# Sixteen kept score units instead of twelve, and q and k loaded as a pair, in a fused top-k attention and MLP kernel

## The chip, the cores and the metric

The kernel runs on one core of one Trainium2 chip. The metric is device time in microseconds for one launch; a time is the median of several runs, and one further execution was taken by the hardware profiler. The engines are named as in the profile: PE is TensorE (matmul), PEld its weight load, DVE is VectorE, ACT is ScalarE, POOL is GpSimd, SP is the engine whose queue issues all DMAs here.

## The reference, cut to what matters

```python
batch, n_heads, seq, head_dim = (8, 8, 576, 64)
scores = scale * np.matmul(q, k.transpose(0, 1, 3, 2))
kth = np.partition(scores, -32, axis=-1)[..., -32:-31]
scores = np.where(scores >= kth, scores, -1000000000.0)
scores = scores - np.max(scores, axis=-1, keepdims=True)
attn = np.exp(scores)
attn = attn / (np.sum(attn, axis=-1, keepdims=True) + 1e-09)
x = (attn @ v)            # (B,H,S,D) -> (B*S, H*D) = (4608, 512)
h = x @ w_in              # 512 -> 2048
return np.maximum(0.01 * h, h) @ w_out   # 2048 -> 512
```

The inputs q, k and v are float32, the weights are float64; the result is (4608, 512) float32.

## The kernel before, in words

**Units.** Two heads of a batch form a pair; there are 32 pairs. A unit is 128 rows of queries of both heads of a pair (or 64 rows of two pairs), with all 576 keys: a score tile `s_sb` of 128 x 2 x 576. There are 144 units, 18 for each of the 8 batches. Whole units run over the pairs of a batch within one block of rows, so units n and n + 8 of a batch lie two blocks apart.

**Steps.** The order of work is written out by hand: `for s in range(len(steps) + LAG + 1)`. Step s runs `top_k` of unit s on DVE, `mask` of unit s - 1 on POOL, `exponents` and `sums` of unit s - 1 on ACT (`ze` at L323), and for unit s - 2 the `reciprocals` on DVE (`rz`, L327), `normalize` on ACT (L330) and `transpose`. `transpose` splits the tile into high and low halves on ACT (`split`, L339), stores each to DRAM (`apart`, L340) and reads it back through a transposing DMA (`wT`, L344). For four units near the start (`HASTY`) the transposition is made by PE instead. Two units' value matmuls (`weigh_values`, L381) come some three to five steps after their top-k; `keep_values` (L395) puts the result into `x`.

**Scores.** At the end of each even step, `scores` makes the scores of units s + 2 and s + 3 on PE (L225) and ACT copies them out (L232). Its PSUM buffers are two called `wide` and one called `narrow`, shared with the early scores below and, the wide ones, with the values.

**MLP.** A chunk of 256 tokens (128 for the first two) becomes ready when all its values are there. Its matmuls (`ph`, L437, and `pz`, L449) are handed out in small portions between the attention parts, by a budget worked out from what is still to be done (`slot_budget`, `mlp_steps`). Before the loop the weights are loaded as words of 16 bits and put together (`round_weights`).

**Kept units.** Some units' scores are made in the first steps and stored to DRAM. `KEPT` lists first unit numbers: for each entry a, the units a, a + 1, a + 8 and a + 9 are kept. `load_early` loads what they need into one `raw` buffer (two k tiles of 288 KB, four q slices of 64 KB); `score_early`, at the end of a step, calls `keep_scores` as often as `EARLY_SCORES` says for that step. `keep_scores` makes one unit's scores on PE (L276) in two score buffers, copies them on ACT (L280) into one of three areas of the MLP's tile `gT`, not yet in use, and stores them (`kept`, L282):

```python
        ps = [ps_sc.tile([P, 2, 512], F32, name="wide", bufs=2) if (2 * k + i) % 3 else
              ps_sc.tile([P, 2, 512], F32, name="narrow") for i in range(2)]
...
        both = gT.rearrange("p f n -> p (f n)")[:, k % 3 * 2 * S:(k % 3 + 1) * 2 * S]
```

Three steps ahead of its top-k, `fetch_scores` (L287) loads a kept unit back, and the even step that would have made its scores skips them.

**q and k loads.** At the end of a step `load_more` decides whether a further pair's q and k may be loaded, and puts both into the list `waiting`, if that list is empty. A later step takes from the list, just after it has issued the transposing transfer, but only where it has no kept unit to fetch (L651).

**DMA.** All DMAs are issued from SP's queue in program order, so an issue that waits holds back those behind it.

Of the kernel before, what the change touches and what calls it, by code (L numbers as in the profile page):

```python
# [20 lines left out]
def kernel(  # L21
# [13 lines left out]
    nc = tc.nc  # L35
# [65 lines left out]
    def load_weights(n):  # L101
        if n >= NPIECE:
            return
        if not AS_WORDS:
            nc.sync.dma_start(piece(n), weights[n])
            return
        raw_of[n] = raws.tile([P, WCH, 4], U16, name="raw")
        flat = raw_of[n].rearrange("p n w -> p (n w)")
        for m, c0, c1 in ROUNDED:
            if m == n:  # L110
                nc.sync.dma_start(flat[:, 4 * c0:4 * c1], weights[n][:, 4 * c0:4 * c1])
# [63 lines left out]
    waiting = []  # L175
# [75 lines left out]
    def load_early(us):  # L251

        raw = raws.tile([P, WCH, 4], U16, name="raw").rearrange("p n w -> p (n w)").bitcast(F32)
        at = 0
        for pi in sorted({u.pairs[0] for u in us}):
            kt = raw[:, at:at + S]
            nc.sync.dma_start(kt, kT[pi])
            at += S
            for u in us:
                if u.pairs[0] == pi:  # L260
                    early_of[u] = raw[:, at:at + P], kt
                    nc.sync.dma_start(early_of[u][0], qT[pi][:, u.q0:u.q0 + P])
                    at += P
# [3 lines left out]
    def keep_scores(u):  # L267

        k = len(kept_of)
        qt, kt = early_of.pop(u)  # L270
        ps = [ps_sc.tile([P, 2, 512], F32, name="wide", bufs=2) if (2 * k + i) % 3 else
              ps_sc.tile([P, 2, 512], F32, name="narrow") for i in range(2)]
        for half in range(2):
            for i, _, side, _ in u.parts:
                d = slice(side * D, (side + 1) * D)
                nc.tensor.matmul(ps[i][:, half, 0:HS], qt[d, :], kt[d, half * HS:(half + 1) * HS],  # L276
                                 start=True, stop=True)
        both = gT.rearrange("p f n -> p (f n)")[:, k % 3 * 2 * S:(k % 3 + 1) * 2 * S]
        for i in range(2):
            nc.scalar.copy(both[:, i * S:(i + 1) * S].rearrange("p (h n) -> p h n", h=2), ps[i][:, :, 0:HS])  # L280
        kept_of[u] = kept.tile([P, 2 * S], F32, name=f"kept{k}")
        nc.sync.dma_start(kept_of[u], both)  # L282
# [217 lines left out]

    steps = units

    KEPT = (24, 40, 56)
    EARLY_SCORES = {0: 4, 1: 2, 2: 1, 3: 2, 4: 1, 5: 2}

    def unit(n):
        return steps[n] if 0 <= n < len(steps) else None
# [26 lines left out]
    with tc.manual_schedule():  # L534
        last = {p: n for n, u in enumerate(steps) for p in u.pairs}

        to_keep = [[steps[n] for n in (a, a + 1, a + 8, a + 9)] for a in KEPT]
        early_units = {u for us in to_keep for u in us}
        to_load, to_keep = list(to_keep), [u for us in to_keep for u in us]
        assert all(len(u.pairs) == 1 for u in to_keep)  # L540

        def score_early(count):

            for _ in range(min(count, len(to_keep))):
                keep_scores(to_keep.pop(0))
                if len(to_keep) % 4 == 0 and to_load:
                    load_early(to_load.pop(0))

        def load_more(s):

            for of, load, n, lag in ((v_of, load_v, LOADED_V, LAG + 1), (qk_of, load_qk, LOADED + 3, 8)):
                if of is qk_of and to_keep:
                    while len(of) < LOADED:
                        load(len(of))
                    continue
                while len(of) < NPAIR and (len(of) < n or last[len(of) - n] + lag <= s):
                    if of is v_of or len(of) < n:
                        load(len(of))
                    else:
                        if not waiting:  # L560
                            load(len(of), at_once=False)
                        break


        for n in range(3):
            load_weights(n)
        jobs = [round_weights(*job) for job in ROUNDED] if AS_WORDS else [iter(())] * len(ROUNDED)
        for n in range(len(jobs) + 1):
            if n == len(jobs) - 1:
                first = first_scores(steps[0])  # L570
                next(first, None)
            for job in jobs[max(n - 1, 0):n + 1][::-1]:
                next(job, None)
            if n == len(jobs) - 1:
                next(first, None)
                load_v(0)
                load_v(1)
            elif n == len(jobs):
                for _ in first_scores(steps[1]):
                    pass  # L580
            if n:
                load_weights(n + 2)
            if n >= len(jobs) - 2:
                load_early(to_load.pop(0))
            if 0 <= n - len(jobs) + HP + 1 < HP:
                load_qk(n - len(jobs) + HP + 1)

        def weights_of(u):
            reciprocals(u)
            normalize(u, 0)  # L590
            normalize(u, 1)

        def values(*place):
            due = [u for n, u in enumerate(steps) if values_at(n) == place]
            if due:
                po = ps_sc.tile([P, 2, 512], F32, name="wide", bufs=2)[:, 0, 0:2 * P]
                po = po.rearrange("p (u n) -> p u n", u=2)
            else:
                return ()
            for n, u in enumerate(due):  # L600
                weigh_values(u, po[:, n, :])
            return [(u, po[:, n, :]) for n, u in enumerate(due)]

        def keep(weighed, *place):
            for u, po in weighed:
                keep_values(u, po)
            attended(*place)

        for s in range(len(steps) + LAG + 1):
            assert s < 7 or not to_keep  # L610
            cur, old, older, new = unit(s), unit(s - 1), unit(s - 2), ()
            if s % 2 == 0:
                new = [u for u in steps[s + 2:s + 4] if u]
            picks = top_k(cur) if cur else iter(())
            budget = slot_budget(s)

            def slot():
                next(picks, None)

            at_first = s < HURRY and s - 2 in HURRIED  # L620
            if at_first:
                weights_of(older)
            slot()
            if old:
                mask(old, 0)
                mask(old, 1)
            late = s < HURRY and not {s - 1, s - 2} & set(HURRIED)
            if older and not late and not at_first:
                weights_of(older)
            mlp_steps(budget)  # L630
            weighed = values(s, MIDDLE)
            at_once = s - 2 in HASTY or any(at == (s, MIDDLE) for at, _ in ready_at)
            if at_once:
                keep(weighed, s, MIDDLE)
            slot()
            if older and late:
                weights_of(older)
            if s - 2 in HASTY:
                transpose_in_haste(older)
            mlp_steps(budget)  # L640
            if old:
                exponents(old, 0)
            mlp_steps(budget)
            if older:
                keep_transposed(older) if s - 2 in HASTY else transpose(older, lambda: mlp_steps(budget))
            if not older or s - 2 in HASTY:
                mlp_steps(budget)
            if unit(s + 3) in early_units:
                fetch_scores(unit(s + 3))
            elif waiting:  # L650
                nc.sync.dma_start(*waiting.pop(0))  # L651
            slot()
            slot()
            mlp_steps(budget)
            if old:
                exponents(old, 1)
                sums(old)
            mlp_steps(budget)
            if not at_once:
                keep(weighed, s, MIDDLE)  # L660
            if new and new[0] in early_units:
                new = ()
            if new and s < HURRY:
                scores(new)
            keep(values(s, END), s, END)
            if new and s >= HURRY:
                scores(new)
            score_early(EARLY_SCORES.get(s, 0))
            budget = slot_budget(s + 1)
            mlp_steps(budget)  # L670
            load_more(s)
        mlp_steps(1e9)
# [58 lines left out]
```

## Time and profile before

| What | Value |
|---|---|
| Time before, median of 3 runs | 1464.72 us (1464.65 to 1465.21) |
| Profiled execution, its own time | 1463.63 us |
| Its span in the profile | 1461.7 us |
| PE busy | 1405.5 us (96%) |
| DVE busy | 1320.3 us (90%) |
| ACT busy | 1100.9 us (75%) |
| POOL busy | 1097.8 us (75%) |
| DMA queue of SP, share of 16 engines | 58.5% |
| kept stores and fetches | 12 and 12, 576 KB each |

The span is the time from the first to the last instruction that was profiled; the execution's own time has 1.9 us around it. Busy shares are averages over stages that differ: the first 61 us are weights, from 61 us on the steps run, and after about 1370 us only MLP work is left. PE's matmuls are pipelined and their ends are modelled, so a busy PE is not PE at its peak; its waits say more than its busy time.

### The profile page before, as it was taken

How to read it: one execution, taken by the hardware profiler on the slowest of the kernel's cores; microseconds unless marked ns; L12 is line 12 of the kernel's file. 1: busy time of each engine (PE TensorE's matmuls, PEld its weight loads, DVE VectorE, ACT ScalarE, POOL GpSimd, SP SyncE). 2: the span in 40 equal slices, each digit the busy share in tenths (PEclk: the TensorE clock that was granted, in tenths of full speed). 3: DMA queues.
4: the chain of work that ended last, by engine and by line, in shares of the span. 5: the costliest groups of instructions: out<-in, count | busy, mean ns of one | idle time of the engine just before them, and what ended most of it. 6: DMA issues, size and time to landing. Idle time of an engine off the chain costs nothing.

```text
span 1461.7 us, 24213 instructions
## 1 busy us (share of the span) xinstructions
PE 1405.5 (96%) x8066; PEld 932.9 (64%) x8068; DVE 1320.3 (90%) x3401; ACT 1100.9 (75%) x1984; POOL 1097.8 (75%) x744
## 2 busy tenths in 40 slices
PE   7848999999989999999999999999999999999998
PEld 2425548576757676767676767676766666666674
DVE  7999999999999999999999999999999999999600
ACT  8878878677868777777778787777777777777710
POOL 3288888878888888888888787888887878787700
PEclk9968999999999999999999999999999999999999
DMA  8967543646576666676656655666566665554510
GB/s 320 344 219 225 140 119 101 194 128 181 151 192 179 172 167 188 156 194 169 157 163 170 169 138 141 171 164 166 149 156 171 164 151 143 153 141 130 150 43 14
DMA packets 394989, 239.03 MB, mean 164 GB/s; under 512 B 334576, under 2 KB 336112, under 8 KB 392944
## 3 DMA queue, kind: packets, MB, share of 16 engines
q1 hardware_dynamic: 394864, 237.48, 58.5%
q8 instruction: 63, 1.03, 0.3%
q14 instruction: 62, 0.51, 0.1%
HBM read 55.77 MB, written 99.09 MB: 106 GB/s over the span
## 4 chain that ended last, share of the span: by engine, by line
PE 77%; DVE 13%; ACT 4%; DMA 4%; issue 1%; SPq 0%; POOL 0%; DVEq 0%; ACTq 0%; POOLq 0%
PE pz L449 30%; PE ph L437 29%; PE wide L381 10%; DVE tops L301 5%; PE wide L225 5%; DVE pairs L304 4%; PE narrow L225 3%; DMA apart<-split 2%; ACT split L339 1%; DVE pairs L296 1%; DMA raw<-in_weights_dram 1%; ACT s_sb L318 1%; ACT s_sb L330 1%; DVE w_out L156 1%; DMA wT<-apart 1%
## 5 line engine op out<-in xcount | busy, mean ns | idle before, releaser
L314 POOL TENSOR_SCALAR pen<-s_sb,tops 128x576 f32<-128x576 f32 x288 | 638.3, 2216 | 203.8 <-DVE tops L301 135.6
L301 DVE MAX8 tops<-pairs 128x8 f32<-128x288 f32 (+1 forms) x1152 | 635.9, 591 | 0.0
L449 PE MATMUL pz<-w_out,gT 128*128 128x512 f32 x1152 | 505.1, 595 | 2.4 <-ACT scale L410 2.4
L437 PE MATMUL ph<-x,w_in 128*128 128x256 f32 x2176 | 482.6, 381 | 0.0
L304 DVE MATCH_REPLACE8 pairs<-tops,pairs 128x288 f32<-128x288 f32 (+1 forms) x864 | 460.1, 538 | 0.0
L437 PEld LDWEIGHTS ph<-x,w_in 128*128 128x128 f32 x2176 | 409.5, 190 | 75.5 <-issue 21.3
L315 POOL TENSOR_TENSOR s_sb<-s_sb,pen 128x576 f32<-128x576 f32 x288 | 406.9, 1413 | 24.0
L449 PEld LDWEIGHTS pz<-w_out,gT 128*128 128x128 f32 x1152 | 216.4, 190 | 266.2 <-issue 261.2
L339 ACT COPY split<-s_sb 128x1152 uint16<-128x1152 uint16 x280 | 309.5, 1146 | 1.7 <-DMA apart<-split 1.7
L330 ACT ACTIVATE s_sb<-s_sb,rz 128x576 f32<-128x576 f32 x288 | 207.7, 773 | 33.4 <-DVE rz L327 33.4
L318 ACT ACTIVATE s_sb<-s_sb,nbias 128x576 f32<-128x576 f32 x288 | 222.4, 772 | 6.4 <-POOL s_sb L315 6.4
L296 DVE TENSOR_TENSOR pairs<-s_sb 128x576 f32<-128x576 f32 x288 | 213.6, 780 | 9.5
L381 PEld LDWEIGHTS wide<-wT,vt 128*64 128x64 f32 x3200 | 161.2, 139 | 53.0 <-issue 36.2
L381 PE MATMUL wide<-wT,vt 128*64 128x128 f32 (+1 forms) x3200 | 179.0, 268 | 10.3 <-DMA wT<-apart 4.7
L443 ACT ACTIVATE gT<-ph 128x512 f32<-128x512 f32 x136 | 80.7, 593 | 58.6 <-PE ph L437 57.7
L395 ACT COPY x<-wide 128x128 f32<-128x128 f32 (+1 forms) x160 | 32.2, 260 | 120.2 <-PE wide L381 120.2
L232 ACT COPY s_sb<-wide 128x704 f32<-128x704 f32 x130 | 98.0, 754 | 20.1 <-PE wide L225 20.1
L458 ACT COPY o_sb<-pz 128x512 f32<-128x512 f32 x36 | 21.1, 585 | 92.3 <-PE pz L449 92.2
L225 PE MATMUL wide<-kt,qt 64*128 64x352 f32 (+1 forms) x360 | 70.4, 507 | 1.0 <-ACT s_sb L247 0.7
L232 ACT COPY s_sb<-narrow 128x448 f32<-128x448 f32 x130 | 62.9, 536 | 1.2 <-PE narrow L225 0.6
L304 DVE MATCH_VALUE_LOAD pairs<-tops,pairs 128x8 f32 x864 | 62.6, 72 | 0.0
L327 DVE RECIPROCAL rz<-ze 128x2 f32<-128x2 f32 x144 | 22.3, 155 | 42.3 <-ACT ze L323 42.1
(67 smaller groups left out, 678.0 us busy)
## 6 DMA issues: line engine op xcount, KB each, us to landing
apart<-split SPq DMA_DIRECT2D x280, 288.0 KB, 2.1
raw<-in_weights_dram SPq DMA_DIRECT2D x15, 1024.0 KB, 6.9
vt<-in_vk_dram SPq DMA_DIRECT2D x32, 320.0 KB, 3.7
out_dram<-o_sb SPq DMA_DIRECT2D x36, 256.0 KB, 2.8
kept<-gT SPq DMA_DIRECT2D x12, 576.0 KB, 3.2
s_sb<-kept SPq DMA_DIRECT2D x12, 576.0 KB, 4.8
qt<-in_qT_dram SPq DMA_DIRECT2D x20, 288.0 KB, 3.5
kt<-in_kT_dram SPq DMA_DIRECT2D x20, 288.0 KB, 3.4
```

Source lines behind the costliest of these rows:

```text
L225: nc.tensor.matmul(to[r0:r0 + u.rows, i, :], qt[d, u.q0:u.q0 + u.rows], kt[d, k0:k1], start=True, stop=True)
L296: nc.vector.tensor_tensor(pairs[:, :, n, :], u.both[:, :, 0:HS], u.both[:, :, HS:S], op)
L301: nc.vector.max(out=u.tops[:, i, r, :], in_=rest[i])
L304: nc.vector.match_replace(out=rest[i], in_to_replace=u.tops[:, i, r, :], in_values=rest[i], imm_value=LOWEST)
L314: nc.gpsimd.tensor_scalar(pen, u.s[i], u.tops[:, i, ROUNDS - 1, 7:8], MASKED, ALU.is_lt, ALU.mult)
L315: nc.gpsimd.tensor_tensor(u.s[i], u.s[i], pen, ALU.add)
L318: nc.scalar.activation(u.s[i], u.s[i], AF.Exp, bias=u.nbias[:, i:i + 1], scale=SCALE, accum_out=u.z[:, i:i + 1])
L330: nc.scalar.activation(u.s[i], u.s[i], AF.Copy, bias=0.0, scale=u.rz[:, i:i + 1])
L339: nc.scalar.copy(split, pairs[:, :, h])
L381: nc.tensor.matmul(po[side * D:(side + 1) * D, o, :], vt[:, c, side, :], u.wT[:, c + side * NKC if c + 1 < NKC else c, r:r + n], start=(c ...
L437: nc.tensor.matmul(ph[:, i, 0:n], w_in[c][:, f * P:(f + 1) * P], x[c][:, 0:n], start=(c == 0), stop=(c == HP - 1),)
L449: nc.tensor.matmul(pz[0:m, 0:DMODEL], gT[:, f, r0:r0 + m], w_out[f // 4][:, f % 4, :], start=(f == 0), stop=(f == NFC - 1),)
```

## The change

The diff adds a fourth entry to `KEPT`, so that the units 72, 73, 80 and 81 are kept too. `EARLY_SCORES` makes sixteen units in steps 0 to 5 in place of twelve: five, four, one, three, one and two, where there were four, two, one, two, one and two. A fourth `load_early` follows in step 0, after the first four units, since `score_early` loads another group whenever the number still to make is a multiple of four. Where a step has no unit to fetch, it now issues all that `waiting` holds, which is the q and the k of one pair, and not one of them.

```diff
-    KEPT = (24, 40, 56)
-    EARLY_SCORES = {0: 4, 1: 2, 2: 1, 3: 2, 4: 1, 5: 2}
+    KEPT = (24, 40, 56, 72)
+    EARLY_SCORES = {0: 5, 1: 4, 2: 1, 3: 3, 4: 1, 5: 2}
...
             if unit(s + 3) in early_units:
                 fetch_scores(unit(s + 3))
-            elif waiting:
-                nc.sync.dma_start(*waiting.pop(0))
+            else:
+                while waiting:
+                    nc.sync.dma_start(*waiting.pop(0))
```

## The prediction

> **What bounds the kernel now.** I read the page first, then the chain of waits, then windows, then single engines. The page's chain by engine says that TensorE (PE) carries the end, with VectorE (DVE) second:
>
> ```profile
> PE 77%; DVE 13%; ACT 4%; DMA 4%; issue 1%; SPq 0%; POOL 0%; DVEq 0%; ACTq 0%; POOLq 0%
> ```
>
> 77% of a span of 1461.7 us is not one stretch. In time order the chain runs through DVE and ACT until about 260 us, alternates until 431, and is nearly pure PE from there. The waits of PE from 432 us to the end (the window cuts the first one, which ends at 431.6) say the same:
>
> ```profile
> PE wide L381 <- DMA wT<-apart: 4.2, 1, 4.2
> PE wide L381 <- DMA vt<-in_vk_dram: 0.3, 1, 0.3
> ```
>
> So after 431.6 us PE work taken away is time taken away, and in the first 140 us PE work is nearly free. What is not free there is ScalarE (ACT). In the chain of the first 140 us, the stretch from 83.5 to 138.3 is ACT, with PE and DMA between its pieces; it ends when ACT's sum (ze) lets DVE's reciprocal go on:
>
> ```profile
> 83.52 0.08 DVE rz L327
> 83.63 1.44 ACT s_sb L330 x2
> ...
> 127.67 6.86 DMA apart<-split
> 134.57 0.04 issue
> ...
> 138.34 0.17 DVE rz L327
> ```
>
> DVE's timeline shows 1.62 us idle before that last reciprocal. The steps before it had 0.7 to 5.3 us between ze and rz, so this is the first time that ACT's lateness stops DVE. From 138 to 206 us DVE runs 8.87 us a step without a gap, so a later start there is a later everything.
>
> **What the skill says.** "DMA: Bandwidth & Descriptors", Queues, rings and completion order: an SDMA engine consumes a ring's descriptors in order. The trace agrees: the last load issued at 74.8 us, behind three v loads and a q, took 5.1 us to land, while a kept store took 2.8 at its shortest. The same page, Specifications, gives about 358 GB/s to HBM per core; the window 61.4 to 74 us shows 325 at a DMA share of 0.91, so that queue is already close to full. "TensorE: Matmul & The Clock Gate", What's actually happening: an idle PE drops to half clock after about 3.4 us. The window 74 to 110 us shows a granted clock of 0.63, so early scores run slower than the same matmuls late.
>
> **Gain.** Units 72, 73, 80, 81 no longer have their scores made at the ends of steps 70 and 78. One pair of units there costs, in the chain:
>
> ```profile
> 308.07 0.79 PE wide L225 x4
> 308.87 0.76 PE narrow L225 x8
> 309.62 0.59 PE wide L225 x4
> ```
>
> That is 2.14 us a pair, 4.28 for two. A check by windows cut at the value matmuls of units 40, 72 and 104, 32 units each; the first has three pairs of kept units (steps 46, 54, 62), the second none:
>
> ```profile
> 467.18:757.07 289.89, 289.89 (x1734) 198.59 (x1733) 283.36 (x738) 226.47 (x419) 240.42 (x161) 1.00 0.65 173
> 757.07:1052.96 295.89, 295.56 (x1777) 202.26 (x1776) 282.08 (x736) 232.79 (x427) 239.10 (x161) 1.00 0.58 157
> ```
>
> 6.00 us over three pairs is 2.00 a pair, with four fetches' traffic and more in it. I take **4.2 us** for two, with 3.2 to 4.6 as bounds. It can be kept only if DVE follows: DVE needs 16 x 8.87 = 141.9 us for steps 72 to 87, and those steps take 148.5 now, so there are 6.6 us of room. The four new fetches (s_sb<-kept, 576 KB, 4.8 us to land) come in steps 69, 70, 77, 78, behind the transposing transfer, and delay the next split store. Units 69 and 77 now have their transposed weights 3.3 us before PE wants them; the units at the same place behind the older fetches (45, 53, 61) have 0.04, 2.4 and 1.4, and PE waited at none of them. That is in the lower bound.
>
> **Early cost.** Step by step, on ACT. An early unit is two copies of 0.64 us; they are 1.18 together, plus PE's turn-round in the three score buffers.
>
> Step 0 gets a fifth unit. Its copies end near 74 us; ACT then idles until 77.1 for GpSimd's mask, which hides it. The fourth early load also comes here: six SP issues of 0.3 to 0.45 us, 832 KB, ahead of three v loads and a q and k which nobody needs before about 111 us. Cost on the path nothing, but these bytes stand in the ring.
>
> Step 1 has four units for two. ACT's timeline now, with the idle at the end:
>
> ```profile
> 78.09 0.62 ACT L280 COPY gT<-wide 128x576 f32<-128x576 f32 x1
> 78.61 0.64 ACT L280 COPY gT<-narrow 128x576 f32<-128x576 f32 x1
> 80.14 0.64 ACT L280 COPY gT<-wide 128x576 f32<-128x576 f32 x1 [0.89 <-PE wide L276]
> 81.08 0.64 ACT L280 COPY gT<-wide 128x576 f32<-128x576 f32 x1 [0.30 <-PE wide L276]
> 83.63 1.44 ACT L330 ACTIVATE s_sb<-s_sb,rz 128x576 f32<-128x576 f32 x2 [1.91 <-DVE rz L327]
> ```
>
> Two units took 3.6 us. The first of the four has its matmuls done early; three more at 1.7 to 1.9 each end near 84.7, so L330 starts 1.1 us late. There is also a wait that is not there now: the stores leave from three buffers in gT, and the fourth unit of step 1 must wait for the landing of the first one's store, issued near 79.4 behind the fifth store, the early load and the v, q, k loads. From 72 us that is 3.6 MB; at 325 GB/s the ring is clear of loads near 83.5, and the store lands near 85. L330 then starts at 86.3, 2.7 late. I take **2.5**; bounds 1.0 and 4.0. Queued behind the waiting copy on ACT are the normalisation, exponents and splits of unit 0, hence SP's stores and DVE's reciprocals of later units.
>
> Step 3 has three units for two: 1.18 of copies and 0.3 of turn-round, **1.5**, bounds 1.2 and 2.0. Step 4 keeps its one unit, but the rotation of score buffers now gives it wide first, narrow second. Today PE begins it only when ACT has freed the narrow buffer (4.5 us idle at 109.47); the wide half can go ahead, one matmul of 0.5 to 0.9 us sooner: **-0.7**, bounds -1.0 and 0. Steps 2 and 5 keep counts; step 5's own copies lie beside SP, which is what ends it.
>
> Sum 2.5 + 1.5 - 0.7 = **3.3 us** of lateness at unit 3's split stores in step 5. SP then issues the transposing transfer, two stores, six q/k loads and the next split store (the 6.86 us landing), all in the same order as now, and rz of unit 6 comes 3.3 later. Earlier reciprocals stop DVE first (slack 2.0 and 0.7 us in steps 4 and 6), which is the same delay, not a second one. Nothing later gives it back: DVE has no idle to use up, and PE waits for these units. Bounds of the sum 1.2 to 6.
>
> **Pairs of q and k.** No bytes are added; the k load moves one step forward, and later pairs up to six steps. Each adds one SP issue of 0.43 us and 288 KB, about 0.8 us of ring, ahead of the next split store. SP's gaps there (it waits 392 us in all for ACT's splits) hide the issue. The tightest units after such a load, 41 and 43, have 1.2 and 1.5 us of slack, so I take **0**; if that cover were gone, up to 0.8 once or twice. A gain from earlier q and k is 0, since L225 never waits for a load. The while loop adds no wait, and GpSimd's queue is untouched.
>
> **Sum.** -4.2 + 3.3 = **-0.9 us**. The profiled execution took 1463.63 (span 1461.7 and 1.9 around it), 1.1 below the median of 1464.72; from it 1462.7, from the median **1463.8**. About 0.2%, 2.9 us, is what a measurement of this kernel can tell from no change.
>
> **Rivals.**
> A. *Tie*, as summed: 1463.8, own range 1461.8 to 1465.6. Chance 0.47.
> B. *The early work is hidden.* The fifth store lands in time and step 3 meets PE turn-round that was idle anyway: lateness 1.2, 1461.7, or 1461.1 with the gain's upper bound. For it: 7.4 us of ACT idle in steps 1 and 2, and a store of 2.8 us if the ring is not full. Against it: most of that idle is PE's turn-round on ACT's own copies and moves with them. Chance 0.35.
> C. *The store buffer becomes the bound*, slower. If the ring in step 1 runs at 200 GB/s, as the 36 us from 74 run on average (212), 3.6 MB last until 90, the store lands at 91.5, L330 starts 9 us late, and the sum is about 9.8 - 4.2: 1470. It decides when that landing is later than 88.8 us, 9.4 after issue; the longest of the twelve stores now took 5.6. Chance 0.11.
> D. *New fetches starve PE* as at 431.6 us, where a fetch and a v load came together: 4.2 us for one of the two pairs, 1468. The v loads lie in steps 72 to 75, not beside them. Chance 0.07.
> That the change does not do what it says is excluded by its order of instructions: sixteen kept stores, four more fetches, pairs of loads.
>
> Range 1460.6 to 1467.0. A falls wholly within 0.2%, apart from its ends; faster 0.36, same 0.45, slower 0.19.
>
> **What would show it.** Right: 16 instructions each in L282 and L287; the last copy of step 1 waiting for a DMA or PE, and L330 of unit 0 starting between 84.5 and 88; rz of unit 6 near 141.6; PE's first unbroken stretch starting near 435; 32 units from the values of unit 72 near 291.8 us. Wrong: rz of unit 6 still at 138 to 139 (B), a copy in step 1 idle for 5 us or more (C), a new PE wait for wT near units 69 to 81 (D).

## The result: slower by 0.4%, and the profile after

| | median | range | runs |
|---|---|---|---|
| before | 1464.68 us | 1461.89 to 1465.85 | 6 |
| after | 1469.73 us | 1467.18 to 1473.69 | 6 |

The ratio is 1.0037, with a 95% interval of 1.0022 to 1.0053: the kernel became 5 us slower where a gain of 0.9 us was forecast, with 1467.0 us as the upper end of the range. A second measurement of the same kernel, among the experiments (e9), gave 1.0027 (1.0016 to 1.0038).

The first profile of after was taken of its slowest execution (1473.69 us, span 1471.9), the second (e9) of one of 1468.34 (span 1466.5). Both are used below.

The page's chain by engine, after, against the first fence of the prediction:

```profile
PE 77%; DVE 11%; DMA 5%; ACT 4%; issue 1%; POOL 1%; SPq 0%; DVEq 0%; POOLq 0%; ACTq 0%
```

PE has the same share; DMA takes a point and DVE gives two. Where the DMA part lies is told by the chain of waits of after, from 79 to 93 us (start, length, what):

```profile
81.63 0.46 ACT gT L280
82.09 7.96 DMA kept<-gT
90.05 0.02 issue
...
90.68 0.65 ACT gT L280
91.32 1.34 ACT s_sb L330 x2
```

A kept store is on the path that sets the end: issued at 82.09, landed at 90.05. ACT's timeline in step 1 shows who stood behind it; the brackets give the idle time before the row and what ended it:

```profile
84.64 0.64 ACT L280 COPY gT<-narrow 128x576 f32<-128x576 f32 x1 [0.30 <-PE narrow L276]
90.14 1.18 ACT L280 COPY gT<-wide 128x576 f32<-128x576 f32 x2 [4.86 <-DMA kept<-gT]
91.21 1.45 ACT L330 ACTIVATE s_sb<-s_sb,rz 128x576 f32<-128x576 f32 x2
```

The fourth early unit of step 1 waited 4.86 us for a free area. Before, L330 started at 83.63 and had waited for DVE; now DVE waits for ACT. DVE's waits from 60 to 160 us, before and then after (second trace), as total, times and longest:

```profile
DVE rz L327 <- ACT ze L323: 1.6, 1, 1.6
```

```profile
DVE rz L327 <- ACT ze L323: 9.5, 6, 2.8
```

The late gain is there. Windows between the value matmuls of units 56, 72 and 88, before and then after (length, then the busy time of PE and the other engines; the last three figures are PE's granted clock, the DMA share and GB/s):

```profile
611.64:757.07 145.43, 145.43 (x818) 99.72 (x817) 141.61 (x369) 113.90 (x209) 119.90 (x81) 1.00 0.63 168
757.07:904.55 147.48, 147.48 (x865) 100.52 (x864) 140.69 (x368) 115.82 (x211) 119.23 (x81) 1.00 0.57 153
```

```profile
624.69:767.98 143.29, 143.29 (x802) 98.28 (x801) 141.29 (x369) 111.52 (x205) 119.72 (x81) 1.00 0.67 178
767.98:914.13 146.15, 145.56 (x850) 99.05 (x849) 140.55 (x368) 113.32 (x207) 119.08 (x81) 1.00 0.60 163
```

2.14 us less in the first and 1.33 in the second, where PE waited 0.59 for the transposed weights of unit 81.

**Where the time went, stretch by stretch.** Each row is the length in one trace less the length in the trace of before, in us. Steps are cut at the first MAX8 of their unit on DVE, values at their first matmul on PE.

| Stretch | after | after, 2nd | pairs alone (e1) | four areas (e3) | fourteen (e11) |
|---|---|---|---|---|---|
| start to step 0 (weights) | +1.5 | +0.3 | +0.7 | -0.4 | +0.6 |
| step 0 to step 9 | **+8.3** | **+8.3** | -1.0 | +4.0 | -1.7 |
| step 9 to step 40 | +0.7 | -1.1 | -1.0 | -0.7 | -1.8 |
| step 40 to values of unit 40 | +1.9 | +1.5 | +0.9 | +1.2 | +1.4 |
| values of units 40 to 56 | +0.6 | -0.1 | +0.1 | -0.1 | -0.1 |
| 56 to 72 | -2.1 | -2.1 | 0.0 | -2.1 | -2.1 |
| 72 to 88 | -1.3 | -1.9 | 0.0 | -1.3 | 0.0 |
| 88 to the end | +0.7 | 0.0 | -0.5 | +0.2 | +0.4 |
| span | +10.2 | +4.9 | -0.9 | +0.7 | -3.3 |

The pairs-alone kernel takes the same time as before, so its column shows what single traces differ by: about 1 us a row. Rows of that size are not explained. The row from step 40 to the values of unit 40 is longer than before in every other trace (0.5 to 1.9 us), also in e12 (+1.6), which has neither more kept units nor pairs of loads: there the one trace of before is short. What stands out is the stretch from step 0 to step 9 and the two kept windows.

**ACT's lateness.** The start of `normalize` (L330) of units 0 to 6 after the first MAX8, less the same before. A normalisation of unit n lies in step n + 2, so column 0 holds what step 1 added, column 2 less column 1 what step 3 added, and so on. Step 1 is the same code in after and e5, and in e3 and e6; their 6.1 and 5.0, 1.8 and 1.2 show how far single traces differ.

| Kernel | 0 | 1 | 2 | 3 | 4 | 5 | 6 |
|---|---|---|---|---|---|---|---|
| after | 6.1 | 6.1 | 8.2 | 7.6 | 9.6 | 9.5 | 9.3 |
| after, 2nd (e9) | 6.2 | 6.2 | 7.7 | 7.2 | 9.3 | 9.5 | 9.2 |
| four areas (e3) | 1.8 | 1.8 | 3.4 | 2.9 | 5.0 | 5.1 | 4.9 |
| loads later (e4) | 2.0 | 2.0 | 3.6 | 3.1 | 5.1 | 5.2 | 5.5 |
| rotation (e5) | 5.0 | 5.0 | 6.8 | 6.2 | 6.2 | 6.8 | 7.3 |
| both (e6) | 1.2 | 1.1 | 3.2 | 2.7 | 2.7 | 2.7 | 2.6 |
| six, three (e7) | 0.0 | 0.0 | 2.1 | 1.5 | 1.5 | 1.4 | 1.2 |
| six, four (e10) | 0.9 | 0.3 | 0.3 | -0.2 | -0.2 | -0.2 | -0.1 |
| fourteen (e11) | 0.0 | 0.0 | 0.0 | 0.0 | -1.5 | -1.9 | -1.6 |

### The profile page after: what moved, and what is told of

It reads as the page before. It is cut to its first block, busy times and chain, and to the rows that moved or that the text cites. A ratio compares the mean times of both kernels' runs of the same rounds, so it can differ in the third digit from the quotient of the medians.

```text
span 1471.9 us, 24274 instructions
## 1 busy us (share of the span) xinstructions
PE 1411.2 (96%) x8066; PEld 936.7 (64%) x8068; DVE 1320.4 (90%) x3401; ACT 1100.6 (75%) x1984; POOL 1096.3 (74%) x744
## 4 chain that ended last, share of the span: by engine, by line
PE 77%; DVE 11%; DMA 5%; ACT 4%; issue 1%; POOL 1%; SPq 0%; DVEq 0%; POOLq 0%; ACTq 0%
PE pz L449 30%; PE ph L437 27%; PE wide L381 10%; PE wide L225 5%; DVE tops L301 5%; DVE pairs L304 4%; PE narrow L225 3%; DMA wT<-apart 2%; DMA raw<-in_weights_dram 2%; ACT split L339 1%; DMA apart<-split 1%; DVE pairs L296 1%; PE ph L405 1%; ACT s_sb L318 1%; ACT s_sb L330 1%
## 5 line engine op out<-in xcount | busy, mean ns | idle before, releaser
L330 ACT ACTIVATE s_sb<-s_sb,rz 128x576 f32<-128x576 f32 x288 | 207.7, 773 | 35.7 <-DVE rz L327 35.7
L381 PEld LDWEIGHTS wide<-wT,vt 128*64 128x64 f32 x3200 | 161.3, 139 | 58.0 <-issue 34.6
L395 ACT COPY x<-wide 128x128 f32<-128x128 f32 (+1 forms) x160 | 32.2, 260 | 122.8 <-PE wide L381 122.8
L225 PE MATMUL wide<-kt,qt 64*128 64x352 f32 (+1 forms) x344 | 68.9, 507 | 5.0 <-ACT gT L280 4.3
```

What stands on the lines that cost most here:

```text
L225: nc.tensor.matmul(to[r0:r0 + u.rows, i, :], qt[d, u.q0:u.q0 + u.rows], kt[d, k0:k1], start=True, stop=True)
L330: nc.scalar.activation(u.s[i], u.s[i], AF.Copy, bias=0.0, scale=u.rz[:, i:i + 1])
L381: nc.tensor.matmul(po[side * D:(side + 1) * D, o, :], vt[:, c, side, :], u.wT[:, c + side * NKC if c + 1 < NKC else c, r:r + n], start=(c ...
```

## The experiments

All ratios are to before, measured beside it. The kernels e1 to e4 shared one chip, e5 to e8 a second, e9 to e12 a third.

**The two halves of the change.** e1 is before with the `while waiting` loop alone; e2 is after with `elif waiting` put back.

> The kernel before with the pair loading alone (twelve kept units as before). Theory S (the loss lies in the first steps, where the fourth early unit of step 1 waits for the store of the first): same as before within 1 us, start of DVE's step 9 unchanged near 144 us after the same weight phase, and the PE distance between the values of units 40 and 72 near 290 us. Rival P (the pairs of loads cost as well: the trace after shows 1.9 us more between steps 42 and 46, where q and k come together): slower by 1 to 3 us, with unit 40 to 48 longer by that.

> The kernel after with the old loading, one of q and k in a step; sixteen kept units as after. Theory S: as slow as after, 5 us over before, with L330 of unit 0 starting 6 us late as in the trace after. Rival P: 2 to 3 us faster than after. A further possibility: later q and k loads, which four more fetch steps push back, come too late for scores; then a PE wait for kt or qt shows near unit 74 or 82 and it is slower than after.

e1: 1.0001 (0.9993 to 1.0009). With twelve kept units the pairs show no cost and no gain, and more than 1.3 us of cost is excluded; rival P's 1 to 3 us do not show. e2: 1.0084 (1.0068 to 1.0101), the slowest of all. It too is late by step 9 (7.2 us, against 8.3 in after); what is added is a wait of PE for a load, in its waits:

```profile
PE narrow L225 <- DMA kt<-in_kT_dram: 4.0, 1, 4.0
```

SP issues two fetches at 705.5 and 714.1 us, the q of the waiting pair only at 722.2 and its k at 729.4; PE waits for that k until 733.1. Values 56 to 72 take 3.6 us more than before in it, not 2.1 less, and 72 to 88 take 1.7 less: with single loads the two windows lose 2.0 us together, where after gains 3.5 and 4.0. The trace is of e2's fastest execution and is 9.1 us longer than before; the ratio says 12, and what the other executions lost is not shown.

**A fourth store area, and later loads.** Both are meant to take the store wait away, by another buffer (e3) and by a shorter queue (e4).

```diff
-        both = gT.rearrange("p f n -> p (f n)")[:, k % 3 * 2 * S:(k % 3 + 1) * 2 * S]
+        if k % 4 < 3:
+            both = gT.rearrange("p f n -> p (f n)")[:, k % 4 * 2 * S:(k % 4 + 1) * 2 * S]
+        else:
+            both = work.tile([P, 2 * NKC - 1, P], F32, name="wT", bufs=3).rearrange("p c n -> p (c n)")
```

```diff
         def load_more(s):
+            if s < 3:
+                return
```

> The kernel after with a fourth store area: the kept scores go round gT's three areas and one buffer of the wT tile, which is not in use until step 2. The fourth unit of step 1 then waits for a store that was issued about 4 us earlier. Theory S: L330 of unit 0 starts some 4 us earlier than after, the time falls by 3 to 4.5 us, to about before. Rival R (the ring and SP's issues are full, the area is only where it shows): the wait moves to the split stores or to the next early units, the time falls by less than 1.5 us.

> The kernel after with the three v loads and the q and k of pair 4 issued at the end of step 3 and not in step 0: 1.57 MB and five issues fewer on the ring ahead of the first store of step 1. Theory S says the store lands about 4 us earlier and the copy behind it starts 4 us earlier: the time falls by 3 to 5 us. Rival R says the same bytes only come later, at step 3, ahead of split stores: falls by 2 us or less. If ACT's copies alone make the lateness (rival A), no change in either this or the fourth area.

e3: 1.0013 (1.0005 to 1.0021). By the ratios to before that is 3.5 us less than the first measurement of after and 2.1 less than the second, whose interval overlaps with it. The trace is clearer: steps 0 to 9 take 4.0 us more than before in place of 8.3, and step 1 on ACT no longer waits for a DMA (three lines more in the code make L280 to L283 and L330 to L333):

```profile
82.71 0.64 ACT L283 COPY wT<-narrow 128x576 f32<-128x576 f32 x1 [0.30 <-PE narrow L276]
83.84 1.26 ACT L283 COPY gT<-wide 128x576 f32<-128x576 f32 x2 [0.49 <-PE wide L276]
84.99 1.44 ACT L333 ACTIVATE s_sb<-s_sb,rz 128x576 f32<-128x576 f32 x2
```

So 4.3 of the 6.1 us of step 1 were the store wait, and 1.8 are copies and turn-round. The stores of step 1 still landed late, 6.0 to 7.3 us after issue in e3 and 7.3 to 8.4 in e10 below, and no copy waited for one. What made the late landing cost time was the area, needed again too soon. e4: 1.0035 (1.0022 to 1.0047), no clear difference to after, though the wait is gone there too (first column 2.0). SP's timeline of e4 shows the five loads ahead of a split store at 110.68, which landed at 116.9, 6.2 us later (2.3 is usual):

```profile
106.50 2.99 SPq L179 DMA_DIRECT2D vt<-in_vk_dram  x3
109.54 0.48 SPq L173 DMA_DIRECT2D qt<-in_qT_dram  x1
110.07 0.51 SPq L173 DMA_DIRECT2D kt<-in_kT_dram  x1
110.68 0.87 SPq L340 DMA_DIRECT2D apart<-split  x2
```

rz of unit 6 then waited 3.5 us for ACT, against 2.1 in e3. Part of what the shorter queue won in step 1 was lost again further on, as rival R had it; steps 0 to 9 took 5.5 us more than before, 4.0 in e3. The trace is of e4's fastest execution (1466.11, the median is 1468.81), and why the others took longer stays open.

**The rotation of score buffers.** e5 is after with one term more, e6 has the fourth area as well:

```diff
-        ps = [... name="wide", bufs=2) if (2 * k + i) % 3 else
+        ps = [... name="wide", bufs=2) if (2 * k + i + (k > 13)) % 3 else
```

> The kernel after with one edit: the rotation of the score buffers is moved on by one from the fifteenth early unit, so that the first early unit of step 5 takes wide and narrow as in the kernel before, and not both wide buffers, of which the values of step 5 hold one. Theory S2 (the lateness is a sum on ACT: store wait 4.3, copies 1.8 in step 1, 1.7 to 2.0 in step 3, 2.0 in step 5 by the rotation): 1.5 to 2.5 us faster than after, 3 us over before. Rival (step 5 lies beside SP's queue, as forecast): within 0.7 us of after.

> Fourth store area and the rotation together. If the terms add: the fourth area's 1465.9 less 2.0, so 1464 and equal to before within 1 us. If the lateness has a floor from SP's issues and the loads, no faster than the fourth area alone.

ACT in step 5 of after (second trace), then of e5:

```profile
125.58 0.41 ACT L395 COPY x<-wide 128x128 f32<-128x128 f32 x2
127.14 0.64 ACT L280 COPY gT<-wide 128x576 f32<-128x576 f32 x1 [1.15 <-PE wide L276]
128.08 0.64 ACT L280 COPY gT<-wide 128x576 f32<-128x576 f32 x1 [0.31 <-PE wide L276]
129.21 0.64 ACT L280 COPY gT<-narrow 128x576 f32<-128x576 f32 x1 [0.49 <-PE narrow L276]
130.05 0.64 ACT L280 COPY gT<-wide 128x576 f32<-128x576 f32 x1 [0.20 <-PE wide L276]
```

```profile
124.23 0.41 ACT L395 COPY x<-wide 128x128 f32<-128x128 f32 x2
124.53 0.65 ACT L280 COPY gT<-wide 128x576 f32<-128x576 f32 x1
125.06 0.66 ACT L280 COPY gT<-narrow 128x576 f32<-128x576 f32 x1
126.04 1.18 ACT L280 COPY gT<-wide 128x576 f32<-128x576 f32 x2 [0.31 <-PE wide L276]
```

The fifteenth early unit takes both wide buffers in after, while the values of step 5 still hold one of the two; PE makes the part in the other buffer and then waits until L395 has emptied that one. PE's line in the second trace of after:

```profile
126.04 1.52 PE L276 MATMUL wide<-raw 64*128 64x288 f32 x5 [1.68 <-ACT x L395]
```

With wide and narrow its scores are ready when L395 ends, and step 5 adds 0.0 instead of 2.0. e5: 1.0021 (1.0014 to 1.0027); the interval overlaps with those of after, so the ratio alone does not show the gain. Nor does the total to step 9, 6.4 us in place of 8.3, show the rotation by itself, since the store wait was 1.1 us shorter in this trace (3.81 us); step 5's own 0.0 does. e6: 0.9998 (0.9988 to 1.0008), equal to before. Both terms are gone in it at once: no copy waits for a store, step 5 adds 0.0, and to step 9 it is 2.2 us late in place of 8.3.

**Where the early units go.** With both mends in place, e7 makes them as 6, 3, 1, 3, 1, 2, e8 as 7, 3, 1, 2, 1, 2, e10 as 6, 4, 1, 2, 1, 2.

> Fourth area, rotation, and one early unit moved from step 1 to step 0, six and three, where ACT has an idle stretch of 2.6 us ahead of the first exponents. Theory S2: ACT's lateness of 1.8 us in step 1 goes, 1.5 us or more faster than the four and rotation kernel, about 1462, below before. Rival R (stores and loads fill the ring; six stores in step 0 land later): the copies of step 0 or 1 wait for a store and nothing is won.

> As the six and three kernel, with seven units in step 0, three in step 1 and two, not three, in step 3. Theory S2: step 3 gives back 1.7 us, step 0's seventh unit costs what does not fit in ACT's idle stretch, about 1 us in step 1; 1461 to 1463. Rival R: the ring is full in step 0, copies wait for stores, 1464 or more.

> Fourth area and rotation, six early units in step 0, four in step 1, two in step 3. Theory S2: step 1 late by 1.2 to 1.8, step 3 not at all; within 1 us of the six and three kernel, a little faster if the 2.1 us of step 3 was more than step 1 costs now. Rival R: step 1's fourth unit waits for a store again and it is 1 us or more slower than six and three.

e7: 0.9991 (0.9983 to 1.0000). Step 1's 1.2 us are gone, the sixth unit of step 0 fits in ACT's idle stretch; 1 us to step 9, not the 1.5 expected, and the intervals of e6 and e7 overlap. e8: 1.0006 (0.9996 to 1.0017). A copy in step 1 waits 2.45 us for a store again (seven stores in step 0). e10: 0.9989 (0.9983 to 0.9996), faster than before.

**Where PE meets the weights.** Behind 460 us PE waited for transposed weights 4.0 us in all in e8, 3.9 in e6 and 1.2 in e10; before did not wait for them there at all. The longest of these waits are at units 65, 69 and 77: 1.19 and 1.66 us at 65 and 69 in e8, 1.82 at 77 in e6, 1.02 at 69 in e10. The lead, from the landing of a unit's `wT` to PE's first value matmul of it, was 3.3 us before at units 69 and 77. At 77 it is 0.0 to 0.7 in all ten traces with sixteen units. At 69 most of the loss is the gain itself: in after PE comes to unit 69 35.8 us after the unit's first MAX8, where it came after 37.9, while the weights land after 35.0, where they landed after 34.6. At 77 the weights also land later, after 35.0 to 36.5 us and in e6 after 38.2, against 34.6 before; but e11, whose fetches do not lie there, has 35.9, so that the new fetches delay them is not shown. What is shown is that PE, made faster, comes close to the landing of the weights, and that a later landing there then costs time.

**Fewer units, and the kernel before with the same care.** e9 is after unchanged. e11 keeps fourteen (not 80 and 81), made as 6, 3, 1, 2, 1, 1 with the fourth area; the fourth `load_early` still follows after the first four units. e12 is before, twelve units made as 6, 3, 0, 1, 1, 1 with the fourth area and the rotation moved from the twelfth unit on.

> The kernel after, unchanged, for a second trace and more times, since its first trace was its slowest execution. Theory S2: about 5 us over before; the copy of the fourth early unit of step 1 waits 3.5 to 5 us for a store; L330 of unit 0 5 to 6 us late, and 7 to 8.5 us by the ninth step. If the store wait of the first trace was an accident of that execution, it is under 2 us here and the time nearer to before.

> Fourteen kept units (72 and 73, not 80 and 81), fourth area, six early units in step 0, three in step 1, one, two, one and one after that. Theory S2: no lateness in steps 1, 3 and 5 (within 0.5 us of before in ACT's normalisations), and the late gain of one pair, 2.1 us: 1.5 to 3 us faster than before, the fastest of all. If the trace of the second pair's smaller gain (1.4 of 2.1 us) tells of a floor by VectorE, little is lost by giving it up.

> The kernel before (twelve units, one load in a step) with the fourth area and its twelve units made six, three, none, one, one, one; the rotation moved on so that step 5 takes wide and narrow. Theory S2: the lateness of 1.7 us that before itself shows at step 8 shrinks; 1 to 1.7 us faster than before. Rival: that lateness comes from the six q and k loads ahead of the split store and stays; within 0.5 us of before.

e9 repeats the store wait (4.97 us) and the 8.3 us to step 9: it was no accident of the first trace. e11: 0.9987 (0.9978 to 0.9996), a median of 1462.01 beside 1464.35 of before; DVE has no wait for ACT between 60 and 160 us, and values 56 to 72 give the 2.1 us. It and e10 are the two whose intervals lie below that of no change; they cannot be told apart. e12: 0.9995 (0.9986 to 1.0003): steps 0 to 9 are 1.7 us shorter, as its theory said, but the time does not show it clearly. Its interval overlaps with those of e10 and e11, so that more kept units beat twelve of the same care is shown by the late windows of the traces and not by the times.

## Why the prediction was wrong

- *What bounds the kernel, and that early lateness goes through to the end*: right. Step 9 is 8.3 us late in both traces of after, and the rows from there to the values of unit 56 add 3.2 and 0.3 us, so nothing gives it back.
- *Gain 4.2 us, bounds 3.2 to 4.6*: 3.5 and 4.0 us in the two traces of after. Right, with up to 0.8 of the second pair's 2.1 lost, as the lower bound had it; that the fetches are the reason, as it said, is not shown. Two readings beside it were off: the window with three pairs holds six fetches, not four, and the sign "32 units from the values of unit 72 near 291.8" could not come, since step 70, where the first pair gains, lies ahead of those values. It measured 294.6 and 293.8, against 295.9 before.
- *Step 1, "I take 2.5; bounds 1.0 and 4.0"*: **this term failed**; it measured 6.1 and 6.2: 4.3 for the store wait, where the forecast has 1.6, and 1.8 for copies and turn-round, where it has 1.1. The mechanism was named, the landing was put too early. The forecast had the load queue clear near 83.5 and the store landed near 85. With step 0's start taken off (1.5 us), the k load landed at 85.9 and the store at 88.6. The mean rate was not the fault: 325 GB/s was assumed, and the window 74 to 90 us of after shows 333 (284 in its first half and 381 in its second, above the 358 that the prediction quotes):

```profile
74.00:90.00 16.00, 8.05 (x34) 4.46 (x30) 15.86 (x42) 6.64 (x13) 13.35 (x10) 0.78 0.98 333
```

  The bytes were. 16 us at 333 GB/s are 5.3 MB; the 3.6 MB counted from 72 us left out the third and fourth stores, still in flight at 74 us (landed at 75.2 and 77.3, 0.6 MB each at most), and the two stores issued behind, of which a part moved before the one ahead had landed. SP was late as well: twelve issues from 74.09 to 81.98 us followed each other, and the store was issued at 82.09, 1.4 us after its copy. The forecast also priced the landing as the cost, where the scarce thing was the area (e3).
- *Step 3, 1.5*: 2.1 and 1.5. *Step 4, -0.7*: -0.5. Right.
- *"Steps 2 and 5 keep counts; step 5's own copies lie beside SP"*: **this step failed.** The counts stay, but the running number k moved by four, so the rotation gave step 5's first unit both wide buffers. It measured 2.0 us, and e5 removed it. The forecast followed the same rotation into step 4, where it gains, and not into step 5.
- *Sum 3.3, bounds 1.2 to 6*: 8.3 us by step 9. With that in the sum, -4.2 + 8.3 = +4.1, near the 5 measured; rz of unit 6 came at 148.2 and 147.0, not near 141.6.
- *Pairs of q and k, 0*: right within 1.3 us (e1). "L225 never waits for a load" held for the kernel before only; without the pairs sixteen units wait 4.0 us (e2).
- *Rivals*: C named the mechanism and the place, at a chance of 0.11. That its 1470 is so near 1469.73 is luck: its cause, a ring at 200 GB/s, did not happen; its threshold, a landing later than 88.8 us or 9.4 after issue, was not reached (88.6 and 8.0; the copy was idle for 4.86 us, not for 5 or more); it had 9 us at L330, where 6.1 came, and nothing in step 5, where 2.0 came. B fell, since rz of unit 6 was over 8 us late. D as stated, 4.2 us of waiting, did not come: behind unit 40 no PE wait for wT is above 0.6 us in the two traces of after. But D had the place right: the leads at units 69 and 77 shrank, and e6, e8 and e10 waited 1.0 to 1.8 us there, for a reason that is in part the gain itself.

## What to carry to other kernels

Work moved into an idle stretch of one engine is priced by the scarcest thing that it passes through: here eight matmuls a unit were nearly free on PE, and the two copies on ACT and the area for the store were not. In e10 stores landed up to 8.4 us after issue and no copy waited, in after they landed up to 8.2 us after issue and a copy waited 4.86: so first ask who needs a transfer's buffer again, and when. Where a landing does decide, count everything in flight when the count starts and what is issued before it ends, and compare the issue time with the queue's own serial time. When a running index selects buffers, adding items shifts every later choice: follow it through all steps, and check who holds the buffer there.

## What was not expected of the hardware

The landing of a 576 KB store ranged from 2.8 to 8.2 us in one trace of after and to 8.6 in the other, and that of a 288 KB load reached 5.9 and 6.3; from 74 to 90 us, where the late ones lie, the DMA share was 0.98. The Trainium skill's "DMA: Bandwidth & Descriptors" (Queues, rings and completion order) says that descriptors are consumed in ring order on each engine, and that completion is not first in, first out for an issuing engine. No landing out of order is shown here: from 74 to 93 us of after the transfers landed in the order of their issue. Overlap is shown: 5.3 MB moved from 74 to 90 us, and the store that landed at 90.05 had at most 4.8 MB in front of it or in it, so by this count some of the two stores behind it had moved by then. The runs do not show engine by engine which bytes went first.
